# Attention with top-32 selection and a GELU network on one core: last query rows turned by DVE and DRAM instead of by TensorE, a seventh scores buffer, in-place sums

## The chip, the cores and the metric

The kernel runs on one core of a Trainium2 chip, as one launch. The metric is the device time of that core in microseconds (us); lower is better.

## What is computed

```python
def _attn_ref(q, k, v):                       # 8 batches, 8 heads, 576 rows, 64 columns, float32
    scores = scale * np.matmul(q, k.transpose(0, 1, 3, 2))
    kth = np.partition(scores, -32, axis=-1)[..., -32:-31]
    scores = np.where(scores >= kth, scores, -1000000000.0)
    scores = scores - np.max(scores, axis=-1, keepdims=True)
    attn = np.exp(scores)
    attn = attn / (np.sum(attn, axis=-1, keepdims=True) + 1e-09)
    return np.matmul(attn, v)
def _moe_ref(x, w_in, w_out):                 # x: (4608, 512), w_in: (512, 2048), w_out: (2048, 512)
    h = x @ w_in
    return (0.5 * h * (1.0 + erf(h / sqrt(2)))) @ w_out
```

The attention output, heads side by side, is the `x` of the second part.

## The kernel before

Work is cut into 144 items. An item is a tile of scores of 128 rows by 2 x 576 keys: for a main item the 128 rows `t` of one pair of heads, for a *last item* (`t == NM`) the last 64 rows of two pairs of heads. Each batch has 16 main items and 2 last items; even batches end with their last items, odd batches begin with them (`items`, `starts`), so four last items stand together: 16 to 19, 52 to 55, 88 to 91, 124 to 127.

The loop `for n in range(ahead)` is one **slot** per item, and it writes each engine's instructions in a fixed order; each engine then runs its own list in that order and waits on semaphores. Slot n holds, by engine:

- PE (TensorE): `scores(n + 2)` (in an even slot also `scores(n + 3)`), `attend` (P times v) of the item or pair three slots back, `transposes(n - 2)` (P turned with 8 + 1 transposes, 8 + 2 for a last item), and between these the pieces of the network (`mlp`): 14 to 18 matmuls per slot, counted out by `room_in`.
- DVE: `top_k(n)`, in whose middle `square_p(n - 2)` may transpose a P tile in 32 x 32 squares, and at whose end `inverse(n - 1)` (L504) is done.
- ACT: copies out of PSUM, GELU, and `softmax(n - 1)` (select L517 and exp L529, one half of the row at a time).
- POOL: `smaller(n + 1)` (L455), `add_small(n - 1)` (L510, "den"), `threshold(n)` (L497, L498), `normalise(n - 1)` (L552), `sum_up(n + 2)` (L447), then up to six small sums of the network (`run_small`).
- SP: `write_p`, `read_p` (a squared P goes through DRAM and comes back turned), loads and stores.

In 48 of the main items P is turned by DVE squares and DRAM (`squared`); all last items are turned by PE. In the steady part (`few[0]`) PE has a single PSUM bank, tag "z", for four uses that follow each other: the last keys (L349) with the turned tail, the product `o`, and `seven`. Whoever is next to write it waits until ACT has copied the previous content out.

The second product of the network runs, for most units, as seven products for eight (`trio_piece`, `seven_piece`). A group takes eight slots (twelve where units of another form stand between). At its start `seven_piece` copies the first `seven` into a new tile `y7` (L945), later ones are added into it on POOL (L950). When the group ends, POOL makes the outputs in six small sums (L979 to L994), of which `lower` (L990) is the last to read `y7`. `y7` has two buffers, so the next group's first copy goes into the other one. In emission order the sums come first: a group's `lower` closes slot 28, 40, 48, 56, 64, 76, ... on POOL, and the next group's first copy stands in slot 33, 41, 49, 57, 69, 77, ... on ACT.

Of the kernel before, what the change touches and what calls it, by code (L numbers as in the profile page):

```python
# [14 lines left out]
def kernel(  # L15
# [95 lines left out]
    def load(n, pair, queue=None, queue2=None):  # L111
        if pair >= n_pairs:
            return
        queue = queue or nc.sync
        queue2 = queue2 or queue
        b, h0 = pair // NP, 2 * (pair % NP)
        src = sources[n]
        if n != "v" and pair >= SQUARES:
            t = flat[n][0]
            for e in range(2):  # L120
                for d in range(2):
                    rows, cols = slice((2 * e + d) * SQ, (2 * e + d + 1) * SQ), slice(d * SQ, (d + 1) * SQ)
                    for at, lo, hi, by in ((0, 0, SM, queue), (SM + e * TL, SM, S, queue2)):
                        by.dma_start(
                            out=t[rows, at : at + hi - lo].rearrange("i (c j) -> i c j", j=SQ),
                            in_=src[b, h0 + e, lo:hi, cols].rearrange("(c i) j -> i c j", i=SQ),
                        )
            return
        t = raw_of(n, pair)
        for e in range(2):  # L130
            queue.dma_start(
                out=t[:, 0:NM, e, :], in_=src[b, h0 + e, 0:SM].rearrange("(t p) d -> p t d", p=P)
            )
            queue2.dma_start(out=t[e * TL : (e + 1) * TL, NM, e, :], in_=src[b, h0 + e, SM:S])
# [141 lines left out]
    def transpose_qk(pair, first=False):  # L276

        q_tail = SM + P
        done = set()

        def squares(c):
            rq, rk, kt = flat["q"][0], flat["k"][0], kt_of.get(pair)
            if c == 0:
                nc.vector.transpose(kt[:, 0:q_tail], rk)
            elif c == 1:
                nc.vector.transpose(kt[:, q_tail:], rq[:, SM:])
            else:
                nc.vector.transpose(q_of[pair], rq[:, 0:SM])

        def by_pe(c):  # L290
            rq, rk = raw_of("q", pair), raw_of("k", pair)
            group = (
                [(rk, j) for j in range(NM)], [(rk, NM), (rq, NM)], [(rq, j) for j in range(NM)]
            )[c]
            tp = bank("tp_qk")
            for x, (r, j) in enumerate(group):
                nc.tensor.transpose(
                    tp[:, x * P : (x + 1) * P], r[:, j].rearrange("p e d -> p (e d)"), ident
                )
            dst = (kt_of[pair][:, 0:SM], kt_of[pair][:, SM:], q_of.get(pair))[c]  # L300
            copy = nc.vector.tensor_copy if first and c < 2 else nc.scalar.copy
            copy(out=dst, in_=tp[:, 0 : len(group) * P])

        def piece(c):
            if c == 0:
                kt_of[pair] = work.tile([P, 2 * P + SM], f32, tag="kt", bufs=NP + 2, name="kt")
            if c == 2:
                q_of[pair] = work.tile([P, SM], f32, tag="qm", bufs=NP, name="qm")
            (squares if pair >= SQUARES else by_pe)(c)
            done.add(c)  # L310
            ahead = 1 if pair >= SQUARES else 2
            if pair + ahead >= SQUARES > pair:
                return
            if c != 0 and done >= {1, 2}:
                load("q", pair + ahead)
            if (c == 0 if pair >= SQUARES else c != 0 and done >= {0, 1, 2}):
                load("k", pair + ahead)

        return [lambda c=c: piece(c) for c in range(3)]

    S_of, stat_of = {}, {}

    def row(i, e):
        return S_of[i][:, e * S : (e + 1) * S]
# [10 lines left out]
    def halves(t, e, step):  # L337

        return spread(t[:, e * TL :], step + (TL if e == 0 else -TL), TL)

# [3 lines left out]
    def last_keys(i, t_ps):  # L344
# [3 lines left out]
        if t < NM:  # L348
            nc.tensor.matmul(  # L349
                t_ps[:, 0:P], lhsT=q_of[pair][:, t * P : (t + 1) * P],  # L350
                rhs=kt_of[pair][:, SM : SM + P], start=True, stop=True,
# [8 lines left out]
        for r in range(2):  # L360
            kt = kt_of[pair + r]
            for e in range(2):
                nc.tensor.matmul(
                    t_ps[half(r, e), r * TL : (r + 1) * TL],
                    lhsT=kt[:, SM + P + e * TL : SM + P + (e + 1) * TL],
                    rhs=kt[:, SM + e * TL : SM + (e + 1) * TL],
                    start=True, stop=True,
                )
        return lambda: nc.scalar.activation(
            s.rearrange("p (r n) -> p r n", r=2)[:, :, SM:S],  # L370
            t_ps[:, 0:P].rearrange("p (r n) -> p r n", r=2), func=AF.Copy, scale=scale,
        )

    def scores(i, second=False):
# [3 lines left out]
        S_of[i] = s = work.tile([P, 2 * S], f32, tag="s", bufs=6, name="s")  # L378
# [3 lines left out]
        if t < NM:  # L382
            q_t, kt = q_of[pair][:, t * P : (t + 1) * P], kt_of[pair]
            for e in range(2):
                rows = slice(e * D, (e + 1) * D)
                nc.tensor.matmul(  # L386
                    s_ps[:, e], lhsT=q_t[rows, :], rhs=kt[rows, 0:SM], start=True, stop=True
                )
# [6 lines left out]
        else:  # L395

            for r in range(2):
                kt = kt_of[pair + r]
                for e in range(2):
                    rows = slice(e * D, (e + 1) * D)  # L400
                    nc.tensor.matmul(
                        s_ps[half(r, e), r, :], lhsT=kt[rows, SM + P + e * TL : SM + P + (e + 1) * TL],
                        rhs=kt[rows, 0:SM], start=True, stop=True,
                    )
            s2 = s.rearrange("p (r n) -> p r n", r=2)
            nc.scalar.activation(s2[:, :, 0:SM], s_ps, func=AF.Copy, scale=scale)
# [129 lines left out]
    def normalise(i):  # L536
# [4 lines left out]
        if i < DIAGS:  # L541
            d = work.tile([P, 2, P], f32, tag="part", bufs=3, name="diag")
# [12 lines left out]
    pt_end = const.tile([P, 2, P], f32, name="pt_end")  # L555
    nc.gpsimd.memset(pt_end, 0.0)

    def squared(i):

        return SINGLE.stop - 2 < i < N - 2 and i % 2 == 0 and items[i][1] < NM and i % RINGS != 12  # L560
# [20 lines left out]
    def read_p(i):  # L581

        if squared(i):
            d = turned.pop(i)
            for k in range(P // SQ):
                nc.sync.dma_start(
                    out=pt_now[0][k * SQ : (k + 1) * SQ, :, 0:P], in_=d[:, :, k, :]
                )

    def transposes(i):  # L590
# [3 lines left out]
        if squared(i):  # L594

            def keys_only(ahead):
                pt_now[0] = work.tile([P, 2 * NM + 1, 2 * P], f32, tag="pt", bufs=1, name="pt")
# [7 lines left out]
        def tails(ahead):  # L605
# [3 lines left out]
            if t % 2 == 0:  # L609
                pt_now[0] = work.tile([P, 2 * NM + 1, 2 * P], f32, tag="pt", bufs=1, name="pt")  # L610
# [7 lines left out]
            elif t < NM:  # L618
                nc.tensor.transpose(tp[:, at : at + P], s[:, SM : S + TL], ident)
            else:  # L620
                for r in range(2):
                    nc.tensor.transpose(
                        tp[0:TL, at + r * P : at + (r + 1) * P],
                        s[:, r * S + SM : (r + 1) * S], ident,
                    )
            if keys:
                keys()
            if t < NM:
                nc.scalar.copy(
                    out=pt_now[0][:, NM, t % 2 * P : (t % 2 + 1) * P], in_=tp[:, at : at + P]  # L630
                )
                return
            for e in range(2):
                c = slice(e * TL, (e + 1) * TL)
                nc.scalar.copy(
                    out=halves(pt_end[c, 0, :], e, P),
                    in_=halves(tp[0:TL, at : at + 2 * P], e, P),
                )

        x = t % 2 * P if t < NM else 0  # L640

        def turn_over(tp, e):
            first = e * (S + TL if t < NM else S)
# [46 lines left out]

    def column(tok):
# [4 lines left out]
    def attend(i):  # L696
# [8 lines left out]
        o = bank("o")  # L705
# [15 lines left out]
        else:  # L721
            for r in range(2):
                vt = raw_of("v", pair + r)
                for j in range(NJ):
                    for e in range(2):
                        nc.tensor.matmul(
                            o[e * D : (e + 1) * D, r * TL : (r + 1) * TL], lhsT=vt[:, j, e, :],
                            rhs=pt[:, r * NJ + j, half(r, e)] if j < NM else pt_end[:, r, half(r, e)],
                            start=(j == 0), stop=(j == NJ - 1),
                        )  # L730
            copies.append(lambda: nc.scalar.copy(
                out=xT[:, at : at + 2, c],
                in_=o[:, 0 : 2 * TL].rearrange("p (r n) -> p r n", r=2),
            ))

        if t == (NM if b % 2 == 0 else NM - 1):
            for r in range(2 if t == NM else 1):
                issue(lambda r=r: load("v", pair + r + NP))
# [59 lines left out]
    def sums(u):  # L798
# [3 lines left out]
        if u == NU - 2:  # L802
            t = work.tile([P, 2 * S], f32, tag="s", bufs=6, name="sum_s")
# [57 lines left out]
    def part_tile():  # L861
        return work.tile([P, HALF], f32, tag="part", bufs=3, name="part")
# [75 lines left out]
    def seven_piece(u):  # L938
# [4 lines left out]
        if j == 0:  # L943
            y7[0] = work.tile([P, HALF], f32, tag="y7", bufs=2, name="y7")
# [9 lines left out]
    def trio_piece(u, names, x):  # L954
# [19 lines left out]
        if k == 1:  # L974
            p2, p5, s7 = end_of["p2"], part_tile(), y7[0]
            end_of["p5"] = p5
# [5 lines left out]
            small.append((1, lambda: pool(y1[:, B2], s7, p5, op=add)))  # L982
            small.append((1, lambda: pool(y0[:, B2], y0[:, B2], p5, op=add)))
            return
# [105 lines left out]

    def room_in(n):
# [6 lines left out]
        return sizes[x] + (1 if x % 2 == 0 else -1)  # L1098
# [55 lines left out]
    for n in range(ahead):  # L1154

        held[0] = n < N and squared(n - 2)
        read_p(n - 3)
# [20 lines left out]
        product = attend(n - 3)  # L1178
# [31 lines left out]
        if few[0]:  # L1210
            softmax(n - 1, 0)
            if n % 2:
                mlp(ODD)
# [65 lines left out]
        if n == 5:  # L1279
            load("q", SQUARES)  # L1280
# [39 lines left out]
```

## Time and profile before

| | |
|---|---|
| median of 3 runs | 1480.3 us (1479.78 to 1480.89) |
| the profiled execution | 1479.73 us, its span 1478.0 us |
| PE busy | 1461.6 us (99%), 8817 records |
| DVE busy | 1294.3 us (88%) |
| ACT busy | 1099.9 us (74%) |
| POOL busy | 1140.1 us (77%) |

Rows of the profile name line, engine, operation, out<-in, and then busy time, mean ns of one, and idle time before it with its cause. A row of a timeline begins with the start (us from the span's start) and the duration; PE durations overlap, so the cost of a PE instruction is read from one start to the next. A float32 matmul leaves two records, a transpose one.

### The profile page before, as it was taken

To read this page: it belongs to the slowest core of one execution; us is meant where nothing else is said; L and a number is where in the kernel's file an instruction comes from. 1 tells how busy PE (TensorE), PEld (TensorE's weight loads), DVE (VectorE), ACT (ScalarE), POOL (GpSimd) and SP (SyncE) were. 2 spreads that over 40 slices of the span, in tenths; PEclk is the share of its full clock that TensorE was granted. 3 is DMA by queue.
4 is the path that set the end of the run, shared out by engine and by line. 5 is a ranking of instruction groups with operands and counts; after the bars stand their busy time and mean duration, and the time that the engine had idled before them with its cause. 6 is when DMAs were issued, how large, how long until landed. Compare 5 with 4: busy or idle time off the path is not lost. (4 is left out here: it accounts for less than half of the span.)

```text
span 1478.0 us, 27006 instructions
## 1 busy us (share of the span) xinstructions
PE 1461.6 (99%) x8817; PEld 1147.9 (78%) x8817; DVE 1294.3 (88%) x3318; ACT 1099.9 (74%) x1942; POOL 1140.1 (77%) x1291
## 2 busy tenths in 40 slices
PE   8999999999999999999999999999999999999999
PEld 6876677877777777887777778787777777787787
DVE  8999899999999988999999987999999997998701
ACT  7999977877777687777777778777777777776620
POOL 6877567877898879877898978886788887987732
PEclk9999999999999999999999999999999999999999
DMA  7424310045435322345534331345453421233300
GB/s 198 143 86 124 84 48 1 24 88 101 95 73 93 66 58 52 65 95 108 105 83 81 69 61 47 66 93 99 97 103 73 89 55 41 61 61 72 70 15 15
DMA packets 477645, 112.94 MB, mean 76 GB/s; under 512 B 413216, under 2 KB 469056, under 8 KB 477504
## 3 DMA queue, kind: packets, MB, share of 16 engines
q1 hardware_dynamic: 476240, 110.78, 35.3%
q8 instruction: 70, 1.15, 0.3%
q14 instruction: 71, 0.58, 0.1%
q10 hardware_dynamic: 1200, 0.39, 0.1%
q0 software_dynamic: 64, 0.03, 0.0%
HBM read 73.39 MB, written 37.75 MB: 75 GB/s over the span
## 5 line engine op out<-in xcount | busy, mean ns | idle before, releaser
L773 PE MATMUL h_ps<-xT,w_in_sb 128*128 128x256 f32 (+1 forms) x2560 | 536.2, 361 | 0.1
L773 PEld LDWEIGHTS h_ps<-xT,w_in_sb 128*128 128x128 f32 x2560 | 436.5, 190 | 73.4 <-issue 25.2
L483 DVE MAX8 top<-lists 128x8 f32<-128x576 f32 (+1 forms) x792 | 476.4, 641 | 0.0
L486 DVE MATCH_REPLACE8 lists<-top,lists 128x288 f32<-128x288 f32 (+1 forms) x528 | 307.9, 589 | 0.0
L552 POOL TENSOR_TENSOR s<-s,rden 128x1152 f32<-128x1152 f32 x135 | 285.8, 2117 | 0.3 <-DVE rden L504 0.3
L529 ACT ACTIVATE s<-s,bias 128x576 f32<-128x576 f32 x288 | 225.4, 787 | 11.0 <-issue 0.4
L517 ACT ACTIVATE s<-s,neg 128x576 f32<-128x576 f32 x288 | 225.5, 793 | 1.7 <-POOL neg L497 1.6
L510 POOL TENSOR_SCALAR den<-den 128x2 f32<-128x2 f32 x144 | 31.4, 218 | 215.9 <-ACT s L529 210.2
L455 POOL TENSOR_TENSOR lists<-lists 128x576 int32<-128x576 int32 x132 | 186.2, 1410 | 4.0
L447 POOL TENSOR_TENSOR lists<-s 128x576 int32<-128x576 int32 x133 | 187.2, 1407 | 0.0
L715 PE MATMUL o<-pt,raw_v 128*64 128x256 f32 x1280 | 153.0, 384 | 1.8 <-ACT s L529 1.1
L715 PEld LDWEIGHTS o<-pt,raw_v 128*64 128x64 f32 x1280 | 87.8, 136 | 85.8 <-issue 37.2
L789 ACT ACTIVATE g<-h_ps 128x512 f32<-128x512 f32 x144 | 78.2, 594 | 100.6 <-PE h_ps L773 100.4
L929 PE MATMUL y_ps<-w_out_sb,sum 128*128 128x256 f32 x472 | 140.4, 379 | 0.0
L394 ACT ACTIVATE s<-s_ps 128x1024 f32<-128x1024 f32 x127 | 125.5, 1035 | 10.5 <-PE s_ps L386 10.3
L664 ACT COPY pt<-tp 128x1024 f32<-128x1024 f32 x85 | 86.6, 1019 | 62.2 <-PE tp L649 62.1
L386 PE MATMUL s_ps<-kt,qm 64*128 64x512 f32 x512 | 129.4, 618 | 0.8 <-ACT s L392 0.8
L504 DVE RECIPROCAL rden<-den 128x2 f32<-128x2 f32 x144 | 23.2, 161 | 108.6 <-POOL den L510 107.4
L486 DVE MATCH_REPLACE8 lists<-first,lists 128x288 f32<-128x288 f32 x264 | 114.3, 439 | 0.0
L929 PE MATMUL y_ps<-w_out_sb,g 128*128 128x256 f32 x480 | 113.4, 379 | 0.0
L483 DVE MAX8 first<-lists 128x8 f32<-128x288 f32 x268 | 106.6, 436 | 0.0
L929 PEld LDWEIGHTS y_ps<-w_out_sb,g 128*128 128x128 f32 x480 | 91.2, 190 | 12.4
(167 smaller groups left out, 2533.1 us busy)
## 6 DMA issues: line engine op xcount, KB each, us to landing
turned<-s SPq DMA_DIRECT2D x192, 144.0 KB, 3.5
pt<-turned SPq DMA_DIRECT2D x192, 144.0 KB, 3.2
raw_v<-in_v_dram SPq DMA_DIRECT2D x64, 128.0 KB, 2.4
out_dram<-y SPq DMA_DIRECT2D x30, 256.0 KB, 2.1
raw_q<-in_q_dram SPq DMA_DIRECT2D x112, 64.0 KB, 2.0
raw_k<-in_k_dram SPq DMA_DIRECT2D x112, 64.0 KB, 2.0
w_out_sb<-in_moe_w_in_dram SPq DMA_DIRECT2D x14, 511.8 KB, 4.8
w_out_sb<-in_moe_w_out_dram SPq DMA_DIRECT2D x10, 511.8 KB, 4.1
```

What stands on the lines that cost most here:

```text
L386: nc.tensor.matmul(s_ps[:, e], lhsT=q_t[rows, :], rhs=kt[rows, 0:SM], start=True, stop=True)
L394: nc.scalar.activation(spread(s, S + TL, SM), s_ps, func=AF.Copy, scale=scale)
L447: nc.gpsimd.tensor_tensor(t[:, :, 1].bitcast(i32), a.bitcast(i32), b.bitcast(i32), op=ALU.add)
L455: nc.gpsimd.tensor_tensor(into_of(i)[:, :, 1].bitcast(i32), both, top, op=ALU.subtract)
L483: nc.vector.max(x[:, e], src[:, e])
L486: nc.vector.match_replace(dst[:, e], x[:, e], src[:, e], LOWEST)
L517: nc.scalar.activation(s, s, func=AF.Prelu, bias=st["neg"][:, e : e + 1], scale=1.0, alpha=STEEP)
L529: nc.scalar.activation(s, s, func=AF.Exp, bias=st["bias"][:, e : e + 1], scale=1.0, accum_out=st["den"][:, e : e + 1],)
L552: nc.gpsimd.tensor_tensor(s, s, wide, op=ALU.mult)
L715: nc.tensor.matmul(o[e * D : (e + 1) * D, 0:n], lhsT=vt[:, j, e, :], rhs=pt[:, e * NJ + j if j < NM else NM, :], start=(j == 0), stop=(j = ...
L773: nc.tensor.matmul(h_tile(u)[:, i, :], lhsT=w_in_sb[:, ko, f * P : (f + 1) * P], rhs=xT[:, ko, c0 : c0 + n], start=(ko == 0), stop=(ko == ...
L929: nc.tensor.matmul(acc[names][:, k], lhsT=lhsT, rhs=rhs, start=(j == 0 and k == 0), stop=(j == FT // 2 - 1 and k == 1),)
```

## The change

- The last items from 52 on (12 of 16) are `squared` too: DVE transposes P, SP writes it to DRAM and reads it back into `pt`. They are `delayed`: their `attend` comes one to two slots later, in the middle of slot 57 and 59 (and 93, 95, 129, 131) or at the start of slot 56 (92, 128). `room_in` moves two pieces of the network from slot 57 to slot 58 (and so on).
- The scores of a last item get the layout of a main one, so that the tails are turned with one transpose instead of two (items 16 to 19), and `pt_end` goes.
- A quarter-load of q or k is one DMA over all 576 rows instead of two (4 per load instead of 8); in k the first or last 64 columns are the tail keys.
- The tails of some v loads are issued by ACT's queue (24 DMAs) instead of SP's.
- Room: "s" gets 7 buffers instead of 6; "part" 2 instead of 3 (`p5` now lies in `y1[:, B2]` and is summed in place); `y7` 1 instead of 2.

The core of the diff (new: `main_keys`, `end_keys`, `both_ends`, `end_rows` give the slices of the new key layout):

```diff
@@ load
-                    for at, lo, hi, by in ((0, 0, SM, queue), (SM + e * TL, SM, S, queue2)):
-                        by.dma_start(
...
+                    queue.dma_start(
+                        out=t[rows, at : at + S].rearrange("i (c j) -> i c j", j=SQ),
+                        in_=src[b, h0 + e, :, cols].rearrange("(c i) j -> i c j", i=SQ),
+                    )
@@ scores, sums
-        S_of[i] = s = work.tile([P, 2 * S], f32, tag="s", bufs=6, name="s")
+        S_of[i] = s = work.tile([P, 2 * S], f32, tag="s", bufs=7, name="s")
@@ squared
-        return SINGLE.stop - 2 < i < N - 2 and i % 2 == 0 and items[i][1] < NM and i % RINGS != 12
+        if not SINGLE.stop - 2 < i < N - 2:
+            return False
+        return items[i][1] == NM or (i % 2 == 0 and i % RINGS != 12)
+    def delayed(i):
+        return squared(i) and items[i][1] == NM
@@ attend
-        o = bank("o")
+        both = delayed(i) and i - 1 in starts
+        o = shared.pop() if both else bank("o")
...
-                issue(lambda r=r: load("v", pair + r + NP))
+                issue(lambda r=r: load("v", pair + r + NP, None, nc.scalar if delayed(i) else None))
@@ part_tile, seven_piece, trio_piece
-        return work.tile([P, HALF], f32, tag="part", bufs=3, name="part")
+        return work.tile([P, HALF], f32, tag="part", bufs=2, name="part")
-            y7[0] = work.tile([P, HALF], f32, tag="y7", bufs=2, name="y7")
+            y7[0] = work.tile([P, HALF], f32, tag="y7", bufs=1, name="y7")
-            p2, p5, s7 = end_of["p2"], part_tile(), y7[0]
+            p2, p5, s7 = end_of["p2"], y1[:, B2], y7[0]
...
-            small.append((1, lambda: pool(y1[:, B2], s7, p5, op=add)))
             small.append((1, lambda: pool(y0[:, B2], y0[:, B2], p5, op=add)))
+            small.append((1, lambda: pool(p5, s7, p5, op=add)))
@@ room_in
-        return sizes[x] + (1 if x % 2 == 0 else -1)
+        return sizes[x] + (1 if x % 2 == 0 else -1) + 2 * (bare(n) - bare(n + 1))
@@ the loop
-        read_p(n - 3)
+        mid = [i for i in (n - 5, n - 4) if delayed(i) and n % 2 and (i % 2 or i in starts)]
+        if not mid:
+            read_p(n - 3)
...
-        product = attend(n - 3)
+        if delayed(n - 4) and n % 2 == 0 and n - 4 not in starts:
+            product = attend(n - 4)
+        else:
+            product = not delayed(n - 3) and attend(n - 3)
...
+            if mid:
+                for i in mid:
+                    attend(i)
+                copy_x()
+                read_p(n - 3)
```

## The prediction

> **What bounds the kernel now.** I read the page's busy shares, then the groups by line, then windows over the slots that the change touches, then timelines of single slots.
>
> ```profile
> span 1478.0 us, 27006 instructions
> PE 1461.6 (99%) x8817; PEld 1147.9 (78%) x8817; DVE 1294.3 (88%) x3318; ACT 1099.9 (74%) x1942; POOL 1140.1 (77%) x1291
> ```
> ```profile
> 524.53:567.54 43.01, 42.99 (x330) 34.78 (x329) 33.67 (x90) 33.92 (x66) 33.66 (x40) 1.00 0.18 36
> 567.54:604.50 36.96, 36.83 (x223) 29.39 (x222) 34.66 (x90) 27.98 (x49) 31.53 (x35) 1.00 0.37 79
> ```
>
> The second fence holds PE's slots 54 to 57 and 58 to 61 (columns: stretch, length, busy time of PE, PE loads, DVE, ACT, POOL, then clock and DMA). PE works without a gap, 42.99 of 43.01 us, while DVE has 33.67 and POOL 33.66. So what PE no longer does comes off the time, and any wait of PE over what it has now is added to it in full: nothing gives it back later.
>
> **What PE loses of work, and what that is worth.**
>
> ```profile
> L649 PE MATMUL tp<-ident,s 128*128 128x128 f32 x696 | 90.4, 273 | 0.0
> L622 PE MATMUL tp_t<-ident,s 128*64 128x128 f32 x32 | 6.1, 273 | 0.0
> ```
> ```profile
> 406.58 1.04 PE L649 MATMUL tp<-ident,s 128*128 128x128 f32 x8
> 407.45 0.60 PE L929 MATMUL y_ps<-w_sum,g 128*128 128x256 f32 x2
> ```
>
> Eight transposes take 407.45 - 406.58 = 0.87 us from start to start, 0.109 us each. Of the 696, 12 items x 8 = 96 go; of the 32 of L622, 24 go with these items, and the four last items that stay with PE need one instead of two, so 4 more. 124 x 0.109 = 13.5 us of PE work in all, 4.4 us in each of the three blocks of last items (slots 54-57, 90-93, 126-129). ACT loses the copies behind them, off the path. The fewer q and k DMAs, and the 24 tail loads on ACT's queue, move no byte more and lie beside PE: I take nothing for them. On SP the read-back of item 56 now stands behind the `attend` in the middle of slot 59:
>
> ```profile
> pt<-turned SPq DMA_DIRECT2D x192, 144.0 KB, 3.2
> ```
>
> It lands in 3.2 us, and its reader comes after some 6 us more of PE's slot 59 and the scores of slot 60; if that cover were gone, PE would wait up to 3 us, in each of three blocks. The tail loads wait on ACT behind such read-backs too, and at worst hold ACT for as long at a slot's end.
>
> **What the change adds: a wait for the one `y7`.** With one buffer, the first `seven` of a group may be copied into `y7` (L945, ACT) only after `lower` of the group before (L990, POOL) has read it. Before, this was free. Slot 41 shows what stands where:
>
> ```profile
> 401.84 0.22 POOL L510 TENSOR_SCALAR den<-den 128x2 f32<-128x2 f32 x1
> 409.12 0.73 POOL L990 TENSOR_TENSOR y<-y,y 128x256 f32<-128x256 f32 x1
> 403.10 0.38 ACT L945 COPY y<-seven 128x256 f32<-128x256 f32 x1
> 403.35 0.80 ACT L517 ACTIVATE s<-s,neg 128x576 f32<-128x576 f32 x1
> 406.28 0.26 ACT L357 ACTIVATE s<-tp_t 128x128 f32<-128x128 f32 x1
> 407.65 1.01 ACT L664 COPY pt<-tp 128x1024 f32<-128x1024 f32 x1 [0.95 <-PE tp L649]
> 405.38 0.38 PE L349 MATMUL tp_t<-kt,qm 128*128 128x128 f32 x2
> 409.27 1.99 PE L386 MATMUL s_ps<-kt,qm 64*128 64x512 f32 x8
> ```
>
> ACT copies at 403.10; POOL is through with `lower` at 409.85. Emission has `lower` in slot 40 and the copy in slot 41, but POOL runs the tail of its slot 40 some 7 us into PE's slot 41. After the change the copy ends at 409.85 + 0.38 = 410.23. Behind it on ACT is the whole softmax of the slot (L517 at 403.35 and on). And `seven` lies in bank "z", whose next writer is PE's L349 at 405.38: it now starts at 410.23, **4.85 us later**. PE does its list in order, so all matmuls of the network behind it wait too. ACT after the copy needs 2.9 us for the softmax half (403.35 to 406.28), 0.3 for small copies and 1.0 for the turned P (L664); that ends at 414.4, and PE with the rest of its slot, 409.27 - 405.38 = 3.9 us, is at 414.1, so nothing much is added behind.
>
> Six groups begin so: slots 41, 49, 77, 85, 113, 121. The last of them:
>
> ```profile
> 1181.18 0.73 POOL L990 TENSOR_TENSOR y<-y,y 128x256 f32<-128x256 f32 x1
> 1174.87 0.38 ACT L945 COPY y<-seven 128x256 f32<-128x256 f32 x1
> 1177.15 0.38 PE L349 MATMUL tp_t<-kt,qm 128*128 128x128 f32 x2
> ```
>
> 1181.91 + 0.38 - 1177.15 = 5.14 us. Six at about 5.0: **+30.0 us**. In slots 21, 33, 69, 105 and 141 other units stand between the groups and `lower` is long done; the copy after the loop (ACT starts it as `lower` ends) costs nothing.
>
> **The three blocks of last items.** Groups begin in slots 57, 93, 129 too, and PE comes there early, having lost its transposes.
>
> ```profile
> 536.76 0.17 DVE L504 RECIPROCAL rden<-den 128x2 f32<-128x2 f32 x1 [1.97 <-POOL den L510]
> 549.07 0.17 DVE L504 RECIPROCAL rden<-den 128x2 f32<-128x2 f32 x1 [4.22 <-POOL den L510]
> 573.39 1.36 DVE L569 STREAM_TRANSPOSE s<-s 128x1152 f32<-128x1152 f32 x1
> 574.68 1.37 DVE L483 MAX8 top<-lists 128x8 f32<-128x576 f32 x2
> 548.82 0.22 POOL L510 TENSOR_SCALAR den<-den 128x2 f32<-128x2 f32 x1 [6.25 <-ACT s L529]
> 559.08 0.22 POOL L510 TENSOR_SCALAR den<-den 128x2 f32<-128x2 f32 x1
> 566.37 0.72 POOL L990 TENSOR_TENSOR y<-y,y 128x256 f32<-128x256 f32 x1
> 561.81 0.38 ACT L945 COPY y<-seven 128x256 f32<-128x256 f32 x1
> 567.54 1.99 PE L386 MATMUL s_ps<-kt,qm 64*128 64x512 f32 x8
> 569.45 0.69 PE L726 MATMUL o<-pt,raw_v 128*64 128x64 f32 x16
> 570.77 2.86 PE L773 MATMUL h_ps<-xT,w_in_sb 128*128 128x256 f32 x12
> 573.46 0.38 PE L349 MATMUL t_ps<-kt,qm 128*128 128x128 f32 x2
> 573.68 4.48 PE L773 MATMUL h_ps<-xT,w_in_sb 128*128 128x256 f32 x20
> 578.00 1.03 PE L927 MATMUL seven<-w_sum,g 128*128 128x256 f32 x4
> 585.70 0.70 PE L386 MATMUL s_ps<-kt,qm 64*128 64x512 f32 x2
> ```
>
> DVE's slot 55 is 549.07 - 536.76 - 4.22 = 8.1 us of work, and each of slots 54 to 57 gets a transpose of 1.3 (573.39 to 574.68). In slot 54 it fits into the 1.97 of idle time, so L504 of slot 54 comes at best at 536.2 and that of slot 55 at 536.2 + 8.1 + 1.3 = 545.6, 3.5 us earlier than now, if ACT, which loses its waits for PE's transposes, keeps up. POOL then works without a gap from one "den" to the next, 559.08 - 548.82 = 10.26 us, and `lower` ends 567.09 - 559.08 = 8.0 behind the second: 545.4 + 10.3 + 8.0 = 563.7. If nothing gets earlier it ends at 567.09. I take 564.0, near the lower end.
>
> PE has its `seven` of slot 57 by about 556 (the copy now starts at 561.81; three sets of transposes, 3.3, and two `attend`, 2.6, no longer stand ahead of it), and its next writer of "z" is then `attend(53)`: it stands some 8 us, to 564.0 + 0.4 = 564.4. From there to the end of slot 59: the rest of slot 57 (20 small products 1.32 = 570.77 - 569.45; 8 products at 0.43 from 578.00 - 573.68 = 4.32 for 10; L349 0.22 = 573.68 - 573.46), 5.0; slot 58 (scores 1.91 = 569.45 - 567.54, 18 products 7.8, L349), 10.0; slot 59 (16 products 6.9, two `attend` 2.6, L349 and 9 transposes 1.2), 10.7: 564.4 + 25.7 = 590.1, against 585.70 now. **+4.4 us** a block (+7.5 with the late end), 4.4 us of removed work already in it: three blocks, **+13.2**.
>
> **What a wait of PE does to its clock.**
>
> ```profile
> 1474.00:1476.00 2.00, 0.37 (x2) 0.00 (x0) 1.18 (x4) 0.00 (x0) 0.00 (x0) 1.00 0.26 93
> 1477.00:1478.00 1.00, 0.00 (x0) 0.00 (x0) 0.00 (x0) 0.00 (x0) 0.00 (x0) 0.53 0.00 0
> ```
> ```profile
> 1.04 4.21 PE L1113 MATMUL warm<-raw_v 128*128 128x128 f32 x18 [1.04 <-DVE raw_v L85]
> L1113 PE MATMUL warm<-ident 128*128 128x128 f32 x276 | 32.7, 275 | 0.0
> ```
>
> PE's last matmul ends at 1474.37, and the granted clock falls to half by 1477.1, 2.7 us later. At the start, 18 records take 4.21 us, 0.234 each, against 32.7 / 276 = 0.118 for the same shape later: half speed for at least 4.2 us, 2.1 us lost. A wait of 5 or 9 us is longer than 2.7, so I expect the clock to fall in each of the nine and to come back within about the 4 us of the start. Bounds: 0 and 2.1 us each; I take 1.6, nearer the upper. 9 x 1.6 = **+14.4**.
>
> [...]
>
> **The sum.** 30.0 + 13.2 + 14.4 = 57.6, less 0.4 for the four single tails in slots 18 to 21: +57.2 us. On the profiled execution's 1479.7 (span 1478.0 and 1.7 around it) that is 1536.9; the median lies 0.6 above that execution: **1537 us**, 3.9% slower.
>
> **Rivals.**
> - *The waits bind, the clock stays.* The page shows no fall inside the run, but in the slots of the windows above PE is idle for 0.15 us in all, so it says little on waits of 5:
>
> ```profile
> PEclk9999999999999999999999999999999999999999
> ```
>
>   Then 1480.3 + 30.0 + 13.2 - 0.4 = 1523. Chance 0.2.
> - *The waits cost more:* `lower` not earlier in the three blocks (3 x 3.1 = 9) and 2.1 us or more of clock each (+5): 1551. Chance 0.11.
> - *Faster: POOL is through with `lower` before PE needs "z".* Then the transposes are what counts: 1480.3 - 13.5 = 1467. It decides in slot 41: `lower` and the copy would have to end by 405.38, not 410.2. POOL's start there is set by "den" at 401.84, and 8.0 us of its list stand between; nothing in the diff moves them. Chance 0.05.
> - *No change:* the two effects would have to cancel, or the new wait be already implied by another. Chance 0.01; the forecast keeps 0.63.
>
> The range takes in the clock's and the blocks' bounds: 1518 to 1554. About 0.2% is what a measurement of this kernel tells from no change. Faster 0.05, same 0.01, slower 0.94.
>
> **What would show it.** Right: in nine places ACT idle before the first copy into `y7`, ended by POOL's `lower`, 5 to 7 us in slots like 41 and 49; PE idle about 5 us (six times) and about 8 us (three times), ended by that copy; PE busy share down to some 95%; granted clock at half after each; PE's transposes 600 instead of 696, DVE's squares 60. Wrong: PE still 99% busy, or those waits below 2 us; a PE wait on read-backs of P or on ACT's loads; a time below 1500.

## The result: 1566.5 us, slower than forecast

| | before | changed kernel |
|---|---|---|
| median | 1480.2 us (1479.8 to 1480.9) | 1566.5 us (1564.7 to 1567.3) |
| ratio | 1 | 1.058, 95% interval 1.056 to 1.060 |
| span of the profiled execution | 1478.0 us | 1563.9 us |

The direction and the main mechanism were right; the time lies above the range (1518 to 1554). The page of the changed kernel (busy time of each engine, then the granted clock in 40 slices):

```profile
span 1563.9 us, 26516 instructions
PE 1471.7 (94%) x8693; PEld 1151.6 (74%) x8693; DVE 1307.9 (84%) x3331; ACT 1082.1 (69%) x1899; POOL 1142.3 (73%) x1290
PEclk9999999999999989999999998999999999899999
```

PE's share fell from 99 to 94%, and its busy time rose although 124 transposes are gone: part of its work now runs at half clock (granted 0.50 and 0.51 in the windows below). What PE waits for (sum, times, longest), in the view of the waits:

```profile
PE tp_t L367 <- ACT y L962: 30.2, 6, 5.0
PE o L738 <- ACT y L962: 29.0, 3, 9.7
PE o L738 <- DMA pt<-turned: 16.2, 3, 5.8
PE o L738 <- ACT p L965: 1.7, 3, 0.6
```

The first two rows are the nine forecast waits for the single `y7`: L962 is ACT's first copy into it, which waited for POOL's `lower` (L1006) in all nine, L367 the last keys, L738 the `attend` of a last item. The third row was not forecast: in slots 59, 95 and 131 PE waits for a read-back of P from DRAM. The four rows make 77.1 us, and the removed transposes 13.5 the other way; of the span's 85.9 there remain 85.9 - 77.1 + 13.5 = 22.3 for the clock (and a few tenths that other waits lost or gained).

Slot 41, as forecast, in timelines of POOL, ACT and PE (start, duration, what, idle time before it and its cause):

```profile
409.29 0.73 POOL L1006 TENSOR_TENSOR y<-y,y 128x256 f32<-128x256 f32 x1
410.05 0.37 ACT L962 COPY y<-seven 128x256 f32<-128x256 f32 x1 [6.93 <-POOL y L1006]
404.85 0.59 PE L946 MATMUL y_ps<-w_out_sb,sum 128*128 128x256 f32 x2
410.47 0.80 PE L367 MATMUL tp_t<-kt,qm 128*128 128x128 f32 x2 [5.03 <-ACT y L962]
```

POOL ends `lower` at 410.02, ACT copies, and PE, idle since 405.44, goes on behind the copy: 5.03 us, where 4.85 was worked out. Its clock, in windows cut at the ends of the half-clock stretches (stretch, length, busy PE, PE loads, DVE, ACT, POOL, clock, DMA share, GB/s):

```profile
405.44:410.03 4.59, 0.00 (x1) 0.00 (x0) 4.59 (x11) 0.00 (x0) 4.51 (x7) 0.99 0.33 85
410.03:413.44 3.41, 2.97 (x10) 2.50 (x11) 0.22 (x1) 3.36 (x7) 2.02 (x2) 0.51 0.42 157
413.44:420.00 6.56, 6.56 (x43) 4.00 (x41) 2.81 (x10) 4.65 (x7) 2.99 (x4) 1.00 0.00 1
567.65:570.38 2.73, 0.00 (x0) 0.00 (x0) 1.64 (x5) 0.72 (x2) 2.57 (x5) 1.00 0.96 150
570.42:580.64 10.22, 3.33 (x42) 3.06 (x43) 7.92 (x20) 3.35 (x6) 8.40 (x9) 0.50 0.30 59
598.10:601.08 2.98, 0.00 (x0) 0.00 (x0) 2.98 (x9) 1.41 (x3) 2.53 (x2) 1.00 0.92 267
601.12:607.90 6.78, 4.80 (x46) 4.27 (x47) 1.70 (x3) 0.37 (x1) 0.00 (x0) 0.50 0.72 109
```

The clock falls 2.7 to 4.6 us after PE's last matmul, just as the wait ends in slot 41, and the half-clock stretch lies on the work behind the wait. Rows four and five are slot 57, the last two slot 59. Now the block of last items, on SP's queue, where the unforeseen wait is made, with the ACT and PE rows that belong to it (a row of a queue: start, time from the first issue of a run to the end of its last, count):

```profile
566.26 3.50 SPq L601 DMA_DIRECT2D turned<-s  x4
569.87 16.60 SPq L134 DMA_DIRECT2D raw_v<-in_v_dram  x4
586.78 2.55 SPq L611 DMA_DIRECT2D pt<-turned  x4
589.75 3.38 SPq L601 DMA_DIRECT2D turned<-s  x4
593.17 2.99 SPq L134 DMA_DIRECT2D raw_v<-in_v_dram  x4
596.26 0.92 SPq L861 DMA_DIRECT2D out_dram<-y  x2
597.27 2.57 SPq L611 DMA_DIRECT2D pt<-turned  x4
584.22 1.12 ACTq L138 DMA_DIRECT2D raw_v<-in_v_dram  x2
577.31 2.40 PE L738 MATMUL o<-pt,raw_v 128*64 128x64 f32 x40 [9.66 <-ACT y L962]
603.10 2.40 PE L738 MATMUL o<-pt,raw_v 128*64 128x64 f32 x40 [5.04 <-DMA pt<-turned]
```

The four loads of v of slot 56 take 16.6 us to issue, where those of slot 57 take 2.99. The waits of SP's queue name the cause:

```profile
SPq L134 <- DMA raw_v<-in_v_dram: 41.2, 3, 14.3
```

In each block an SP load stands some 14 us (41.2 in the three, 14.3 the longest) until another load of v has landed. In this one it is the fourth SP load of slot 56: it leaves at 586.1, just as the first tail load on ACT's queue lands, issued at 584.22 for slot 57 and 1.8 us on its way. Between SP's third load at 571.7 and that one no load of v is issued. ACT's load stands behind the copy into `y7` (576.89). Everything on SP is late by that, up to the read-back of item 55, issued at 597.27 and read by PE at 603.10.

### The profile page after: what moved, and what is told of

It is laid out like the page before. It is cut to its first block, busy times and chain, and to the rows that moved or that the text cites. A ratio compares the mean times of both kernels' runs of the same rounds, so it can differ in the third digit from the quotient of the medians.

```text
span 1563.9 us, 26516 instructions
## 1 busy us (share of the span) xinstructions
PE 1471.7 (94%) x8693; PEld 1151.6 (74%) x8693; DVE 1307.9 (84%) x3331; ACT 1082.1 (69%) x1899; POOL 1142.3 (73%) x1290
## 5 line engine op out<-in xcount | busy, mean ns | idle before, releaser
L946 PE MATMUL y_ps<-w_out_sb,sum 128*128 128x256 f32 x472 | 143.6, 387 | 0.0
L410 ACT ACTIVATE s<-s_ps 128x1024 f32<-128x1024 f32 x127 | 125.1, 1032 | 14.8 <-PE s_ps L402 14.7
L946 PE MATMUL y_ps<-w_out_sb,g 128*128 128x256 f32 x480 | 119.3, 393 | 0.0
L672 ACT COPY pt<-tp 128x1024 f32<-128x1024 f32 x73 | 74.4, 1019 | 55.9 <-PE tp L657 55.8
L946 PEld LDWEIGHTS y_ps<-w_out_sb,g 128*128 128x128 f32 x480 | 94.6, 199 | 14.2
```

Of the source, the lines that this page charges most:

```text
L410: nc.scalar.activation(spread(s, S + TL, SM), s_ps, func=AF.Copy, scale=scale)
L946: nc.tensor.matmul(acc[names][:, k], lhsT=lhsT, rhs=rhs, start=(j == 0 and k == 0), stop=(j == FT // 2 - 1 and k == 1),)
```

## The experiments

All ratios are to the kernel before, timed beside each run (1480.0 to 1480.4 us).

**The single `y7` alone, in the kernel before**

```diff
-            y7[0] = work.tile([P, HALF], f32, tag="y7", bufs=2, name="y7")
+            y7[0] = work.tile([P, HALF], f32, tag="y7", bufs=1, name="y7")
```

> The kernel before with one edit: y7 gets one buffer instead of two. Theory (the one buffer makes ACT's first copy wait for POOL's sum, PE for ACT, and the clock falls in each wait): six waits of PE of 5.0 us that cost 6.7 us each with the clock, and in slots 57, 93 and 129, where PE comes no earlier than before, three of 3.9 us that cost about 5.6 each: 40 + 17 = +57 us, 1537 us. Rival (the wait hurts only together with the rest of the change, because there PE comes early and the queues are tied): no wait over 1 us in slots 41 and 49, 1480 to 1485 us.

1539.8 us, ratio 1.040 (1.039 to 1.042). One row of its waits holds the cause, nine times:

```profile
PE tp_t L349 <- ACT y L945: 40.9, 9, 5.0
```

Of 58.7 us more span, 40.9 are waits; the other 18 are put down to the clock, 2.0 for each wait.

**The nine waits taken out of the changed kernel**: the seventh piece's sum and its scratch tile, one buffer each, change roles with every group, so the room stays as it is.

```diff
-    y7 = [None]
+    y7, roles = [None], ["p7", "y7"]
...
         if j == 0:
-            y7[0] = work.tile([P, HALF], f32, tag="y7", bufs=1, name="y7")
+            roles.reverse()
+            y7[0] = work.tile([P, HALF], f32, tag=roles[0], bufs=1, name="y7")
...
-        t = work.tile([P, HALF], f32, tag="p7", bufs=1, name="p7")
+        t = work.tile([P, HALF], f32, tag=roles[1], bufs=1, name="p7")
```

> The changed kernel, y7 and p7 (each one buffer) change roles from group to group, so that the first copy of a group goes into the buffer of the last p7, which POOL has read long before; no more memory, all else as in the change. Theory (the lost time hangs on the y7 wait, and the late read-backs in slots 59, 95, 131 follow from it): no wait of PE over 1 us is left in the nine places, the clock stays at 1.0, and of the 13.5 us of transposes saved some 8 to 12 are won: 1469 to 1473 us. Rival A (the late read-back of P has its own cause, the loads of ACT's queue that SP waits for): slots 59, 95, 131 keep 5 us each and their clock loss, about 1490 to 1495. Rival B (the added DVE squares hold PE back): 1476 to 1484.

1493.1 us, ratio 1.009 (1.007 to 1.010): 73 us of the changed kernel's 86 came from this buffer, directly or through what it delayed. But the kernel is still slower than before:

```profile
PE o L738 <- DMA pt<-turned: 12.9, 3, 4.4
```

The read-back stays late without the `y7` wait, as rival A had it.

**The tail loads on SP's queue, in the changed kernel**

```diff
-                issue(lambda r=r: load("v", pair + r + NP, None, nc.scalar if delayed(i) else None))
+                issue(lambda r=r: load("v", pair + r + NP, None, None))
```

> The changed kernel, but the tails of the v loads stay on SP's queue. Theory (in slot 56 SP's fourth v load waits for a semaphore that a tail load of ACT's slot 57 sets; that one comes late behind the y7 wait, and with SP stands the read-back of item 55): SP is not held for 14 us, the waits of 5.0 to 5.8 us in slots 59, 95, 131 and their clock loss go, 3 x 8.5 = 25 us: 1541 us; the nine y7 waits stay. Rival (the read-back is late because DVE's squares and the writes are late by themselves): 1560 to 1567 us, the waits stay.

1542.6 us, ratio 1.042 (1.041 to 1.044). The read-back waits of the last items are gone from the view of the waits, the nine for `y7` stay (30.0 and 28.8 us). So ACT's queue carried the delay, worth 24 us with its share of the clock. That did not yet say that nothing else would make the read-back late: here PE, held 9.6 us by `y7` two slots earlier, comes late itself.

**The waits filled with matmuls that nobody reads, in the changed kernel**

```diff
+        warm = pair_tile("fill")
+        for _ in range(count):
+            nc.tensor.matmul(warm[:, 0, 0:P], lhsT=ident, rhs=ident, start=True, stop=True)
...
```

(The calls: 23 in slots 41, 49, 77, 85, 113, 121; 45 ahead of `attend` in 57, 93, 129; 23 between the two in 59, 95, 131.)

> The changed kernel with idle matmuls of the identity put where PE waits: 23 (about 4.9 us) before the last keys in slots 41, 49, 77, 85, 113, 121, 45 (9.6 us) before the product in slots 57, 93, 129, 23 between the two products in slots 59, 95, 131; their output is not used. They take the place of the waits and keep PE busy. Theory (the time over the waits themselves is the half clock after them): the granted clock stays at 1.0 and the time falls by what slots 41 and the like lost beyond the wait, 12.5 + 6.2 + 8.4 = 27 us: 1539 us. Rival (that excess is a chain of waits on ACT and POOL, and the low clock only goes with it): no gain, 1565 to 1570 us.

1545.6 us, ratio 1.044 (1.042 to 1.046). The clock never falls inside the run, and 1566.5 - 1545.6 = 20.9 us come back: the price of the half clock over twelve waits, in line with the 22.3 that remained above. I had expected 6 us more from it.

**Both causes taken away**: the roles exchanged, the tail loads on SP.

> The change with both waits taken away at their cause: the seventh piece's sum alternates between its two buffers (as in the run with the roles exchanged) and the second half of v is loaded on SP's queue instead of ScalarE's. My theory: the two are all that stands against the 124 removed transposes (13.5 us). The nine waits for the buffer are gone, the three late read-backs too; what is left is per block 0.6 us before the second attend (ScalarE's copy of P) and up to 2 us of small waits, and the clock stays at full speed. 1480 - 13.5 + 3 x (0.6 to 2.6) = 1468 to 1475, I take 1472, half clock under 10 us in all. Rival A: the late read-back of the last items has a cause of its own beside the queue of the tail loads (SP's own backlog, now with two more loads in it): PE waits 3 us or more in three blocks, each with a stretch of half clock, 1488 or more. Rival B: the squares on VectorE hold back its exponentials' sums and PE is slowed all over the blocks by many small waits: 1480 to 1490 with no wait over 1 us.

1492.2 us, ratio 1.008 (1.006 to 1.009): rival A. With PE no longer late, the read-back is late again (of the eight loads of slot 56 and the eight of slot 57 one row each is shown):

```profile
560.27 0.47 SPq L138 DMA_DIRECT2D raw_v<-in_v_dram  x1
561.15 2.94 SPq L611 DMA_DIRECT2D pt<-turned  x4
564.20 3.41 SPq L601 DMA_DIRECT2D turned<-s  x4
567.66 0.89 SPq L134 DMA_DIRECT2D raw_v<-in_v_dram  x1
573.19 1.00 SPq L861 DMA_DIRECT2D out_dram<-y  x2
574.25 2.60 SPq L611 DMA_DIRECT2D pt<-turned  x4
579.63 2.40 PE L738 MATMUL o<-pt,raw_v 128*64 128x64 f32 x40 [4.14 <-DMA pt<-turned]
```

From 550 to 577 SP issues one DMA behind another with hardly a gap. Its queue is the bound: between the write of P of item 55 (564.20) and its read-back (574.25) stand eight loads of v and a store. The kernel before has in the same stretch of slots one write and one read-back per two slots:

```profile
567.12 1.05 SPq L844 DMA_DIRECT2D out_dram<-y  x2
574.82 3.40 SPq L579 DMA_DIRECT2D turned<-s  x4
580.89 2.55 SPq L586 DMA_DIRECT2D pt<-turned  x4
592.35 3.26 SPq L579 DMA_DIRECT2D turned<-s  x4
```

**The same, without the eight loads of slot 57**

```diff
-            for r in range(2 if t == NM else 1):
+            for r in range(2 if t == NM and not (delayed(i) and i % 2) else 0 if t == NM else 1):
```

> As the run with both causes taken away, but the eight loads of v that follow the attend of slot 57 (two pairs of the next batch) are left out, so the rows of v used there are those of an older batch; the order on PE is that of the change. It asks what sets the late read-back. My theory: SP's queue, which issues one DMA after another (0.5 to 0.9 us each): eight loads and a store stand between the write of P and its read-back, 567.66 to 574.25. Without the loads the read-back issues some 3 us earlier at least (it waits for the write to land, about 3 us after its last issue at 567), so the wait of 4.1 us shrinks to 1 us or less: 1473 to 1479. Rival: the read-back waits for the write itself, whose square on VectorE comes late, and the loads only fill the time: the wait stays at 3 us or more, 1488 or more.

1475.2 us, ratio 0.997 (0.995 to 0.998). The read-back issues 3.4 us earlier and PE stands 0.71:

```profile
564.01 3.43 SPq L601 DMA_DIRECT2D turned<-s  x4
567.54 1.61 SPq L861 DMA_DIRECT2D out_dram<-y  x2
570.84 2.54 SPq L611 DMA_DIRECT2D pt<-turned  x4
576.07 1.39 PE L738 MATMUL o<-pt,raw_v 128*64 128x64 f32 x40 [0.71 <-issue]
```

From the issue of the read-back to the start of `attend` it is 5.4 us with the loads (579.63 - 574.25) and 5.2 without (576.07 - 570.84), so the transfer did not get faster with fewer bytes beside it; it was issued earlier. This is the test of the cause: same squares, same write, fewer issues ahead of the read-back, and 17 us less (1492.2 - 1475.2), more than all the removed transposes.

**Network products moved between the two `attend` of slot 59** (on the run with both causes away)

```diff
+                    if len(mid) == 2 and i == mid[1]:
+                        mlp(ODD + 3)
                     attend(i)
...
-            if n % 2:
+            if n % 2 and len(mid) < 2:
                 mlp(ODD)
```

> As the run with both causes taken away, and in each block of last items five of the six products of the second layer that followed the second attend stand between the two attends of slot 59: the same matrix products, in another order. My theory: the 4.1 us before the second attend are only the time to the landing of the read-back, so 4.3 us of products ahead of it cover them, and the 3.41 to 6.83 us of half clock behind them go too. Left per block are 0.6, 1.0 and 0.5 us. 1480 - 13.5 + 3 x 2.1 = 1473, range 1471 to 1478: faster than before. Rival A: the read-back comes later in step with PE (its write waits for work that PE sets off), so a wait of 3 us or more stays: 1485 or more. Rival B: the copy of the attended rows, now 4 us later, holds up slot 60, which reads them: a new wait there of 2 us or more, 1480 to 1488.

1486.5 us, ratio 1.004 (1.003 to 1.006), where 1473 was expected: the wait goes from slot 59 and a shorter one comes in slot 60 (2.8, 2.5 and 1.3 us in the three blocks), since SP's queue is as full as it was and the next read-back is late too. In the second block:

```profile
939.41 4.05 PE L727 MATMUL o<-pt,raw_v 128*64 128x256 f32 x20 [2.53 <-DMA pt<-turned]
```

**Slot 57's loads on ACT's queue** (on the run with both causes away): only the four tails, or all eight. If SP's issues set the late read-back, four issues of about 0.6 us fewer bring PE's wait from 4.1 us to 1.7, and eight do more.

```diff
-load("v", pair + r + NP, None, None)
+load("v", pair + r + NP, None, nc.scalar if delayed(i) and i % 2 else None)   # four tails
+load("v", pair + r + NP, nc.scalar if delayed(i) and i % 2 else None)         # all eight
```

> As the run with both causes taken away, but of the eight loads that follow the attend of slot 57 the four second halves go on ScalarE's queue, and SP keeps four; nothing is left out. [...] 1480 - 13.5 + 3 x (2.0 + 1.7) = 1478, range 1475 to 1482. Rival: the loads on two queues wait for one another again as in the change, and the wait stays at 4 us: 1488 or more.

> As the run with both causes taken away, but all eight loads that follow the attend of slot 57 go on ScalarE's queue; nothing is left out. My theory: SP's queue is then as in the run without these loads (read-back issued at 570.8, wait 0.7 us, 1475). ScalarE has idle stretches of 2.7 and 2.2 us in these slots and issues eight loads at some 0.6 us each, so its next activations come up to 2 us later and cost PE up to 1 us per block: 1475 to 1479, faster than before or level with it. Rival: ScalarE's queue is in the way (its exponentials wait behind loads that wait for the attend, and PE for their sums): a new wait of 3 us or more in slots 58 to 60, 1486 or more.

Both expectations were missed: 1502.2 us (ratio 1.015, 1.013 to 1.016) and 1506.8 us (1.018, 1.016 to 1.019). Fewer issues on SP made it later. SP's longest wait of this kind, first with four, then with eight loads on ACT:

```profile
SPq L138 <- DMA raw_v<-in_v_dram: 6.2, 1, 6.2
```
```profile
SPq L134 <- DMA raw_v<-in_v_dram: 9.6, 1, 9.6
```
```profile
563.66 0.40 SPq L134 DMA_DIRECT2D raw_v<-in_v_dram  x1
560.86 0.38 ACTq L134 DMA_DIRECT2D raw_v<-in_v_dram  x1
```

In the second, SP's loads of slot 56 begin at 563.66, after the first of ACT's loads of slot 57, issued at 560.86, has landed. These are different pairs of heads. This is the wait of 14.3 us again, here 9.6 and made by moving one line: that SP's loads wait for loads of ACT's queue is shown; through what, no run shows. PE's three waits for read-backs grew from 11.4 us to 20.7 and 18.9. With all eight loads on ACT, PE also waits 6.7 us in three places for ACT's copies of scores (L410), which stand behind these issues; that part is as the rival had it.

**The fourth last item back to PE** (on the run with both causes away): item 55, 91, 127 is turned by PE, the other three keep squares and DRAM.

```diff
-        return items[i][1] == NM or (i % 2 == 0 and i % RINGS != 12)
+        if items[i][1] == NM:
+            return i - 1 not in starts
+        return i % 2 == 0 and i % RINGS != 12
...
-        return squared(i) and items[i][1] == NM
+        return SINGLE.stop - 2 < i < N - 2 and items[i][1] == NM
```

> As the run with both causes taken away, but the fourth of the last items of each block (55, 91, 127), whose read-back came late, gets its P turned by PE again, in slot 57, as the kernel before did; the other three keep squares and DRAM. SP loses eight of its issues between the loads of slot 57 and slot 59, and one write and read-back less means 93 of the 124 transposes stay removed (10.1 us). My theory: the late read-back was the only large wait left, so what stays is 2.0 us per block (0.6, 1.0 and 0.5): 1480 - 10.1 + 6 = 1476, range 1474 to 1481, no half clock. Rival A: the transposes in slot 57 need bank z or the one buffer of turned P while these are taken, and PE waits there for 2 us or more: 1482 to 1490. Rival B: the first attend of slot 59 (item 54) now waits for its own read-back, which stands behind the same loads: 1485 or more.

1474.5 us, ratio 0.996 (0.995 to 0.998): faster than both kernels, by 5.7 us and by 92. Its page, and slot 59 in its timeline:

```profile
span 1472.5 us, 26549 instructions
PE 1451.2 (99%) x8720; PEld 1134.8 (77%) x8720; DVE 1304.1 (89%) x3328; ACT 1084.9 (74%) x1905; POOL 1142.3 (78%) x1290
PEclk9999999999999999999999999999999999999999
```
```profile
574.24 2.55 PE L740 MATMUL o<-pt,raw_v 128*64 128x64 f32 x80 [0.58 <-ACT p L968]
```

PE is at 99% again, both `attend` of slot 59 run as one stretch of 80 records, and what stands ahead of them is 0.58 us for ACT's copy.

## Why the prediction was wrong

- **PE is the bound, a wait of PE is time lost** (right). The experiments turned waits into time at one to one, plus the clock.
- **Removed work, 13.5 us** (not contradicted). It was not measured by itself. In the last run 97 of the 124 transposes are gone (27 come back, nine for each of three items; PE has 97 records less than before), not 93 as its expectation says: 10.6 us by the same row. It gains 5.7, with 1.2 us of small waits in each block and 1 to 2 us elsewhere against it. What the seventh buffer for "s" and the fewer loads of q and k are worth was not measured apart.
- **Six waits of about 5.0 us for the single `y7`** (right): 30.2 against 30.0 us.
- **Three blocks, +4.4 us each** (the `y7` wait right, the block as a whole not). In the changed kernel slot 54 of PE begins, and POOL's `lower` runs, at

```profile
537.47 1.99 PE L402 MATMUL s_ps<-kt,qm 64*128 64x512 f32 x8
576.12 0.73 POOL L1006 TENSOR_TENSOR y<-y,y 128x256 f32<-128x256 f32 x1
```

  `lower` ends 39.38 us behind the start of slot 54 (forecast 564.0 - 524.53 = 39.47, before the change 42.56), and `attend` starts 39.84 behind it (forecast 39.87): POOL was earlier by what was worked out. The wait is 9.66 us and not 8 because PE came to it 1.3 us earlier than "about 556". But from the start of slot 54 to that of slot 60 a block got 14.6 to 15.4 us longer. Of the 10.2 us above 4.4 in the first block, 5.6 are the two waits ahead of the `attend` of slot 59 (0.58 and 5.04, the next point) and about 4 are clock (half of the 3.33 and 4.80 us of work in the half-clock windows above), of which 1.6 stood in the clock's own term.
- **"I take nothing for them"** (the step that failed). The tail loads on ACT's queue were priced as bytes and as work beside PE, and the one read-back that I looked at, that of item 56, had 6 us of cover. Two things were left out. ACT's tail loads stand behind the forecast `y7` wait on ACT, and SP waits until one of them has landed (41.2 us in the three blocks). And the read-backs of the last items themselves, 55 above all, stand on SP behind twice the writes and read-backs and the loads of v. PE waited 16.2 us for read-backs and 1.7 for the copy ahead of them. I had written "up to 3 us, in each of three blocks" as what lost cover would cost; it was 5.0 to 5.8 us and clock, and it was in no rival.
- **Clock, 9 x 1.6 = 14.4 us** (that it falls in the waits: right; too small): 20.9 us by the filled run, 22.3 by what remains of the span, over twelve waits and not nine, 1.7 to 1.9 each. The single buffer alone gave 2.0 each. The half clock lasted 3.41 to 10.24 us (last section), where about 4 were expected.

The sum: forecast 57.2, span longer by 85.9. The 28.7 between are 17.9 for the read-backs and the copy, 7.9 for the clock (22.3 - 14.4), and 2.9 for the `y7` waits (59.2, where 30.0 + 13.2 - 0.4 and the 13.5 of removed work give 56.3). The range's upper end, 1554, had only the clock's and `lower`'s bounds in it; with the 3 us per block that the text named it would have reached 1563.

## What to carry to other kernels

Where a change puts DMAs on a second engine's queue, list what that engine waits for ahead of them and look in the waits of the other queue for their landing: here an SP load of slot 56 stood some 14 us for a load on ACT's queue that comes later in the program. Count the issues of a queue in the slots of a change, here 0.5 to 0.9 us each, as one counts an engine's work; a read-back has cover only if the queue reaches it in time (issued 3.4 us earlier, it cost PE 0.71 us and not 4.14). And a delay that hides behind a larger one is not gone: take the larger one away before pricing it.

## What the runs showed of the hardware

In the changed kernel, by its records of the granted clock, the half clock came inside the run in twelve stretches, four of 3.41 us, five of 6.83 and three of 10.24 (the windows above are cut to within 0.1 us of them). Their begins lie whole multiples of 3.41 us apart: from 410.03 to 570.42 it is 47 times that, and from there to 601.12 nine more. What ran at half clock behind a wait differed from place to place: 2.97 us of work behind the wait of slot 41, 3.33 behind that of slot 57, 4.80 behind the last of slot 59. A shorter wait than these had such a stretch behind it too: in the run with products between the two `attend`, a wait of 2.53 us was followed by

```profile
936.88:939.41 2.53, 0.00 (x0) 0.03 (x1) 1.80 (x6) 2.21 (x4) 1.98 (x4) 1.00 0.51 129
940.00:943.40 3.40, 3.40 (x19) 1.88 (x15) 3.40 (x9) 0.00 (x0) 3.32 (x5) 0.50 0.02 5
```

with PE at work before and after. PE's waits for POOL ahead of the turned tails (L637) in the changed kernel, four of at most 1.7 us, had none: from 7.30 to 410.00, where they lie, the granted clock was 1.00. Where the limit lies stays open.
